# A Fourier mixing layer ahead of an MLP: twiddle factors inside the first stage's weights, and the second stage by even and odd frequencies on eight strips of the array

## The chip, the cores and the metric

The kernel runs on one core of a Trainium2 chip, in fp32 throughout. The metric is the device time of one execution in microseconds (us). Before the change it is 2734.07 us, the median of three runs (2733.72 to 2735.22).

The engines are called by their names or as the profile has them: TensorE (PE, its weight loads PEld), VectorE (DVE), ScalarE (ACT), GpSimd (POOL) and SyncE (SP), which issues most of the DMAs.

## What is computed

A global filter over the sequence in the frequency domain, followed by a two-layer MLP with a hard-swish:

```python
X = np.fft.rfft(x, axis=1)                    # x: 8 x 3008 x 256
y = np.fft.irfft(X * (filt_r + 1j * filt_i), n=3008, axis=1)
h = y.reshape(24064, 256) @ w_in              # 256 x 2048
out = (h * np.clip(h + 3, 0, 6) / 6) @ w_out  # 2048 x 256
```

## The kernel before

**The MLP and its steps.** The 24,064 tokens are cut into 47 blocks of 512 (`BLK`), the hidden width into eight parts of 256 (`NP`). Block 0 runs in a plain form while the weights are still being converted. For blocks 1 to 46 each part is one *step*: `up_1` to `up_5` make seven half-size products of 256 columns (one level of Strassen's scheme, `product`, L518), VectorE and ScalarE combine them and apply the hard-swish (L544, L549, L563, L568), `g_sums` makes the sums of the second product (L575 to L578), and `down` (L594) makes seven products in fourteen matmuls one step later. `out_1` to `out_5` add up and store a finished block. That makes 46 x 8 = 368 steps.

**The Fourier transform.** 3008 is 47 x 64, so a transform has two stages with twiddle factors between them. It is done batch by batch for batches 1 to 7, inside the steps of earlier blocks:

- `a_unit` (L349), eight per batch: the first stage, over the 47 rows of four columns of each half of the 64 columns. Four matmuls of 47x64 weights and 512 columns, on four tiles of the array (two halves of the rows, two of the columns), into two PSUM banks. ScalarE copies both banks to `t1` (L352), and `z_store` (L361) writes them to `z_tmp` in DRAM.
- `t2_load` (L365) reads `z_tmp` back in another order. `b_unit` (L372), twelve per batch, is the second stage for two of 24 indices: two full 128x128 matmuls of 256 columns into one bank. Its weights `wb` hold cosines with the twiddle factors in them, a different table for each index, and so are loaded for each batch again (`table_load`, L190) along with the filter `ft` (L187, L189).
- `f_unit` (L389 to L391) multiplies by the filter on VectorE straight from PSUM: three operations, four (L387) in batch 1. `y_unit` (L407, L408) makes the complex sum with two more, on VectorE, or in batch 1 on GpSimd (L404, L405).
- `bi_unit` (L419), six per batch: the first stage back, for four indices: four matmuls of 64x64 on 512 columns into two banks, copied by ScalarE (L422) into `t3` and written by `g_store` to `g_tmp`.
- `n_unit` (L472): the last stage, of up to five groups of 94 tokens; `t4_load` fetches its input, ScalarE copies the result into the token buffer `xn` (L478), and `t_sums` (L511) makes sums of it on GpSimd.

Batch 0 is transformed at the start in a form of its own.

**What sets the order.** There is one instruction stream per engine, written out by hand. `at(step, fn, ...)` puts a unit into a plan; the main loop emits, for each step, `up_1`, then the units that are in `EARLY` (the four with matmuls: `a_unit`, `b_unit`, `bi_unit`, `n_unit`), then the rest of the step, and at its end all other units (`f_unit`, `y_unit`, loads, stores). So a unit's matmuls stand behind `up_1`, and its VectorE work stands at the end of the step, ahead of the next step's `hswish`. `places(n)` says at which steps the units of batch n stand, `n_at` where the `n_unit`s do. For batches 2 to 7 the `b_unit`s of a batch stand two steps apart, `a_unit`s in four of eight steps.

**Buffers.** All of `a_unit`, `b_unit`, `bi_unit` and `n_unit` take their PSUM banks from one pool of two, in turn (`psF`, names `psf` and `psn`). `t1` has two buffers, `t2` three, `t3` two (`T3B`), `wb` two.

Of the kernel before, what the change touches and what calls it, by code (L numbers as in the profile page):

```python
# [10 lines left out]
FP32 = mybir.dt.float32  # L11
I32 = mybir.dt.int32
AXT = mybir.ActivationFunctionType
ALU = mybir.AluOpType
PSUM = bass.MemoryType.PSUM

# [4 lines left out]
N = 3008  # L23
NA = 47
# [12 lines left out]
NT = KH // TC  # L37
TB = 3
FB = 2
T3B = 2  # L40
NU = KH // 2
NP = DFF // 256
TOK = 2 * NA
# [12 lines left out]
def _make_tables():  # L56
    a = np.arange(NA)
    c = np.arange(NC)
    wa = np.zeros((P, P))
    wai = np.zeros((P, HC, TOK))  # L60
    start = np.zeros((P, 2 * P))
    for h in range(2):
        for k in range(KH):
            th = 2 * np.pi * ((a * k) % NA) / NA
            for g in range(2):
                wa[h * 64:h * 64 + NA, g * 64 + k] = np.cos(th)
                wa[h * 64:h * 64 + NA, g * 64 + 32 + k] = -np.sin(th)
            start[h * 64:h * 64 + NA, P + 4 * k + h] = np.cos(th)
            start[h * 64:h * 64 + NA, P + 4 * k + 2 + h] = -np.sin(th)
    wb = np.zeros((P, KH, P))  # L70
    wi = np.zeros((P, 3, NC))
    re, im = slice(0, NC), slice(NC, P)
    for k in range(KH):
        for q in range(64):
# [8 lines left out]
    for q in range(64):  # L83
        g, sign = (q, 1.0) if q < 32 else (31 - q, -1.0)
        co, si = (f([2 * np.pi * ((j * g) % NC) / NC for j in range(HC + 1)]) for f in (np.cos, np.sin))
        ab = np.concatenate([co, np.zeros(HC - 1) if q == 63 else si[1:HC]])
        wi[q, 0], wi[HALF + q, 0] = ab, sign * ab
        wi[q, 1], wi[HALF + q, 1] = ab, -ab
        wi[q, 2], wi[HALF + q, 2] = sign * ab, sign * ab
    start[:, :P] = np.eye(P)  # L90
# [17 lines left out]
            th = 2 * np.pi * (((k + NA * q if q < 32 else NA * (q - 31) - k) * n) % N) / N  # L108
            direct[q, k - KH + TC], direct[HALF + q, k - KH + TC] = 2 / N * np.cos(th), -2 / N * np.sin(th)
    f = np.float32  # L110
    return wa.astype(f), (wai / N).astype(f), wb.astype(f), wi.astype(f), start.astype(f), direct.astype(f)


@with_exitstack
def kernel(
# [8 lines left out]
):  # L124
    nc = tc.nc

    wa_np, wai_np, wb_np, wi_np, start_np, direct_np = _make_tables()
    wa_d = nc.inline_tensor(wa_np, name="wa_t").ap()
    wai_d = nc.inline_tensor(wai_np, name="wai_t").ap()
    wb_d = nc.inline_tensor(wb_np, name="wb_t").ap()  # L130
    wi_d = nc.inline_tensor(wi_np, name="wi_t").ap()
    start_d = nc.inline_tensor(start_np, name="start_t").ap()
    direct_d = nc.inline_tensor(direct_np, name="direct_t").ap()


    z_d = nc.dram_tensor("z_tmp", (B, KH, P, D), FP32, kind="Internal").ap()
    g0_d = nc.dram_tensor("g0_tmp", (NC, 2, KH, D), FP32, kind="Internal").ap()
    g_d = nc.dram_tensor("g_tmp", (B, NU, 2, 2, NC, D), FP32, kind="Internal").ap()

    def pool(name, bufs, **kw):  # L140
        return ctx.enter_context(tc.tile_pool(name=name, bufs=bufs, **kw))
# [1 line left out]
    const = pool("const", 1)  # L143
    t1p = pool("t1p", 2)
    t2p = pool("t2p", TB)
    tabp = pool("tabp", FB)
    sp = pool("sp", 2)
    yp = pool("yp", 3)
    t3p = pool("t3p", T3B)
# [7 lines left out]
    psU = pool("psU", 1, space=PSUM)  # L157
    psO = pool("psO", 1, space=PSUM)

    wa = const.tile([P, P], FP32, name="wa")  # L160
    wai = const.tile([P, HC, TOK], FP32, name="wai")
    wi = const.tile([P, 3, NC], FP32, name="wi")
    xs = const.tile([P, 3, XC, D], FP32, name="xs")
    ft = [const.tile([P, TC, D], FP32, name="ft%d" % i) for i in range(FB)]
    t4 = const.tile([P, 2 * NJ, D], FP32, name="t4")
# [12 lines left out]
    def table_load(b, c):  # L178
        if b == 0 and c >= FB:

            at = x0_at(1536 * (c - FB), 1536)
            t, wb = at[:, 0:1024].rearrange("p (k d) -> p k d", k=TC), at[:, 1024:].rearrange("p (k m) -> p k m", k=TC)
        else:
            t, wb = ft[(b * NT + c) % FB], tabp.tile([P, TC, P], FP32, name="wb")
        st["ft", b, c] = t
        for src, p0 in ((filt_r, 0), (filt_i, HALF)):
            nc.sync.dma_start(t[p0:p0 + 32, :, :].rearrange("p k d -> p (k d)"),  # L187
                              raw(src, c * TC, [[NA * D, 32], [1, TC * D]]))
            nc.sync.dma_start(t[p0 + 32:p0 + 64, :, :], raw(src, NA - c * TC, [[NA * D, 32], [-D, TC], [1, D]]))  # L189
        nc.sync.dma_start(wb, wb_d[:, ts(c, TC), :])  # L190
        st["wb", b, c] = wb
# [148 lines left out]

    def a_unit(b, c):
        xc = xs[:, (b * NB + c) % 3, :, :]
        t = t1p.tile([P, 2, XC // 2, D], FP32, name="t1")
        ps = [bank(b) for h in range(2)]
        for g in range(2):
            for h in range(2):
                nc.tensor.matmul(ps[h][ts(g, 64)], wa[ds(h * 64, NA), ts(g, 64)],  # L349
                                 xc[ds(h * 64, NA), 2 * g:2 * g + 2, :], start=True, stop=True)  # L350
        for h in range(2):
            nc.scalar.activation(out=t[:, h, :, :].rearrange("p j d -> p (j d)"), in_=ps[h], func=AXT.Copy)  # L352
        st["t1", b, c] = t

    def z_store(b, c, q=nc.gpsimd):
        t = st.pop(("t1", b, c))
        for g in range(2):
            for ri in range(2):
                p0 = g * 64 + ri * 32
                z = z_d[b, :, ts(ri, NC), :].rearrange("k (h j) d -> k h j d", h=2)  # L360
                q.dma_start(z[:, :, ds(c * XC + 2 * g, 2), :], t[p0:p0 + KH, :, :, :])  # L361

    def t2_load(b, c):
        t = t2p.tile([P, TC, D], FP32, name="t2")
        nc.sync.dma_start(t, z_d[b, ts(c, TC), :, :].rearrange("k p d -> p k d"))  # L365
        st["t2", b, c] = t

    def b_unit(b, i):
        c, r = divmod(2 * i, TC)
        ps = bank(b).rearrange("p (u d) -> p u d", u=2)  # L370
        for u in range(2):
            nc.tensor.matmul(ps[:, u, :], st["wb", b, c][:, r + u, :],  # L372
                             st["t2", b, c][:, r + u, :], start=True, stop=True)
        st["ps", b, i] = ps
# [37 lines left out]
    def bi_unit(b, i):  # L412
        ys = [st.pop(("y", b, i + v)) for v in range(2)]
        ps = [psF.tile([P, 2, D], FP32, name="psf", tag="f") for ri in range(2)]
        for v, ri in ((0, 0), (1, 0), (0, 1), (1, 1)):

            products = isinstance(ys[v], tuple)
            w, y = (wi[:, 1 + ri, :], ys[v][ri]) if products else (wi[ts(ri, 64), 0, :], ys[v][ts(ri, 64)])
            nc.tensor.matmul(ps[ri][ts(v, 64)], w, y, start=True, stop=True)  # L419
        t = t3p.tile([P, 2, 2, D], FP32, name="t3")  # L420
        for ri in range(2):
            nc.scalar.activation(out=t[:, ri, :, :], in_=ps[ri], func=AXT.Copy)  # L422
        st["t3", b, i] = t
# [260 lines left out]
    with tc.manual_schedule():  # L684
# [82 lines left out]
        direct(NU - 2)  # L767
        direct(NU - 1)
        load_bits(6)
        nc.sync.dma_start(wa, wa_d)  # L770
        n_first()
        g_store(0, NU - 4)
        for c in range(2):
# [3 lines left out]
        convert(3)  # L777

        def wai_load():
            nc.sync.dma_start(wai[:, 8:HC, :], wai_d[:, 8:HC, :])  # L780

        at(0, bi_unit, 0, NU - 2)
# [10 lines left out]
        at(2, x_load, 1, 2)  # L793

        n_at = {0: -2, 1: -2}
        used = {}
        stored = 0
        for i in range(2, len(chunks)):
            k = token(i)[0] // BLK
            head = chunks[i][1] == 0  # L800
            n_at[i] = s = (k - 1) * NP + (6 if head or k in used else 3)
            used[k] = 1
            if head:
                stored = s - 3 + (k == first[1])
            at(max(stored, n_at[i - 2] + 1), t4_load, i)
            for dh in range(2):
                at(s + dh, n_unit, i, dh)

        def places(n):
            k = first[n]
            u = [NU - 1 - i for i in range(NU)]
            b_at = [(k - 2 - j // 3) * NP + 6 - 2 * (j % 3) for j in u]

            bi_at = [b_at[i] + (5 if i % 6 == 1 else 3) for i in range(NU)]
            a_at = [(k - 7 + c // 4) * NP + (0, 2, 5, 7)[c % 4] for c in range(NB)]
            if n == 1:
                a_at = list(range(2, NB + 2))  # L820
                b_at = [12, 13, 14, 18, 19, 20, 21, 22, 26, 27, 28, 29]
                bi_at = [i + 3 for i in b_at]
            return a_at, b_at, bi_at

        prev = None
        for n in range(1, B):
            a_at, b_at, bi_at = places(n)
            for c, s in enumerate(a_at):
                at(s, a_unit, n, c)
                at(s, z_store, n, c, nc.sync if n == 1 else nc.gpsimd)  # L830
                if c >= 3:
                    at(max(a_at[c - 3], s - 6), x_load, n, c)
                elif n > 1:
                    at(max(prev[c + NB - 3], s - 6), x_load, n, c)
            for c in range(NT):
                s = b_at[2 * (c - TB) + 1] + 1 if c >= TB else a_at[-1] + 1
                at(s, t2_load, n, c)
                s = b_at[2 * (c - FB) + 1] + 1 if c >= FB else a_at[-1 if n > 1 else 3] + 1
                at(s, table_load, n, c)
            for i in range(NU):  # L840
                at(b_at[i], b_unit, n, i)
                at(b_at[i], f_unit, n, i)
                at(b_at[i] + 1, y_unit, n, i)
                if i % 2:
                    at(bi_at[i], bi_unit, n, i - 1)
                    at(bi_at[i], g_store, n, i - 1)
            prev = a_at


# [97 lines left out]
```

## Time and profile before

| | |
|---|---|
| median of three runs | 2734.07 us |
| the profiled execution's own time | 2733.72 us |
| its span, first to last instruction | 2731.9 us |
| granted TensorE clock | 0.998 |
| first step of block 1 begins | 141.15 us |
| HBM read / written | 120.86 MB / 71.93 MB |

The groups of the transform, as the page's list by line and shape has them (busy time is the union of a group's intervals; an fp32 matmul counts as two instructions):

| line | operation | count | busy us | mean ns |
|---|---|---|---|---|
| L349 | PE, `a_unit`, 47x64, 512 columns | 448 | 67.6 | 615 |
| L372 | PE, `b_unit` of batches 1 to 7, 128x128, 256 columns | 336 | 87.5 | 383 |
| L419 | PE, `bi_unit` of batches 1 to 7, 64x64, 512 columns | 336 | 48.8 | 614 |
| L472 | PE, `n_unit`, 128x128, 94 columns | 1000 | 126.2 | 272 |
| L352 | ACT, copies of `a_unit` | 112 | 60.8 | 595 |
| L389, L390, L391 | DVE, filter products of batches 2 to 7 | 72 each | 49.3, 49.1, 50.0 | 684, 683, 695 |
| L407, L408 | DVE, complex sums of batches 2 to 7 | 72 each | 49.5, 49.6 | 687, 689 |

A profile line of the timeline has the start and the length in us, the engine, the line of the kernel, the operation, the tiles written and read, shapes and a count of merged neighbours; in brackets stands how long the engine was idle ahead of it and what ended that.

### The profile page before, as it was taken

Reading aid. Unit: us, or ns where it says so; the run is one execution under the profiler, and the core shown is the slowest. Engines: PE = TensorE matmul, PEld = TensorE weight load, DVE = VectorE, ACT = ScalarE, POOL = GpSimd, SP = SyncE. Lnnn points to the kernel's source line nnn. Section 1 sums busy time; section 2 is a strip of 40 time slices with the busy share of each in tenths; the row PEclk is TensorE's granted clock in tenths of the full one; section 3 lists DMA queues with packets and bytes.
Section 4 is the critical chain, followed back from the end, with each engine's and each line's share of the span. In section 5 each row is a group of like instructions: output and inputs, shape, how many; then the busy total and the mean of one; then the engine's idle time right before and its main releaser. Section 6 shows DMA issues by size and latency. Waiting matters only on the chain.

```text
span 2731.9 us, 47123 instructions
## 1 busy us (share of the span) xinstructions
PE 2699.5 (99%) x18110; PEld 2400.5 (88%) x18110; DVE 1953.9 (72%) x3395; ACT 1328.3 (49%) x2662; POOL 423.7 (16%) x622
## 2 busy tenths in 40 slices
PE   8999999999999999999999999999999999999998
PEld 6488889998899988999889998899988989999997
DVE  7968756787567875678757777577775777766665
ACT  3344454445544455444554444544455454444443
POOL 2433321001210012100121001210012000100000
PEclk9999999999999999999999999999999999999999
DMA  8632233212332123321233212332123321100000
GB/s 234 198 106 83 55 85 89 72 50 56 85 92 68 50 57 92 100 63 41 61 88 98 70 40 57 91 93 70 40 60 90 91 73 39 42 24 24 19 9 16
DMA packets 119645, 195.88 MB, mean 72 GB/s; under 512 B 21561, under 2 KB 82681, under 8 KB 119105
## 3 DMA queue, kind: packets, MB, share of 16 engines
q1 hardware_dynamic: 101663, 148.19, 18.9%
q0 software_dynamic: 17152, 44.23, 7.0%
q8 instruction: 143, 2.34, 0.4%
q14 instruction: 81, 0.66, 0.1%
q10 hardware_dynamic: 606, 0.46, 0.1%
HBM read 120.86 MB, written 71.93 MB: 71 GB/s over the span
## 4 chain that ended last, share of the span: by engine, by line
PE 94%; DVE 4%; DMA 1%; issue 1%; ACT 0%; SPq 0%; POOL 0%; POOLq 0%; DVEq 0%
PE po L594 42%; PE al L518 23%; PE be L518 17%; PE psn L472 4%; PE psf L372 2%; PE psf L419 2%; PE psf L349 2%; DVE s L387 1%; DVE g L568 1%; PE po L318 1%; PE po L372 0%; DVE y L243 0%; DVE y L254 0%; DVE y L256 0%; DVE w_all L259 0%
## 5 line engine op out<-in xcount | busy, mean ns | idle before, releaser
L594 PEld LDWEIGHTS po<-w_all,g 128*128 128x128 f32 x10304 | 1368.1, 191 | 142.2 <-issue 38.1
L594 PE MATMUL po<-w_all,g 128*128 128x128 f32 x10304 | 1399.4, 276 | 0.8 <-DVE g L568 0.6
L568 DVE SCALAR_TENSOR_TENSOR g<-r,h 128x512 f32<-128x512 f32 x736 | 511.8, 695 | 275.2 <-ACT r L563 263.5
L563 ACT ACTIVATE r<-h,half_c 128x512 f32<-128x512 f32 x736 | 531.0, 721 | 330.8 <-DVE h L544 318.7
L518 PE MATMUL al<-xt,w_all 128*128 128x256 f32 x2208 | 660.4, 381 | 3.9 <-DVE h L549 3.4
L518 PE MATMUL be<-xn,w_all 128*128 128x256 f32 x1472 | 437.8, 379 | 0.0
L544 DVE TENSOR_TENSOR h<-be,s 128x512 f32<-128x512 f32 x368 | 254.1, 691 | 252.1 <-PE be L518 242.3
L518 PEld LDWEIGHTS al<-xt,w_all 128*128 128x128 f32 x2208 | 335.3, 192 | 6.5 <-DVE h L549 4.7
L518 PEld LDWEIGHTS be<-xn,w_all 128*128 128x128 f32 x1472 | 279.7, 190 | 37.9
L558 ACT ACTIVATE h<-al 128x256 f32<-128x256 f32 x368 | 141.0, 383 | 347.5 <-PE al L518 347.5
L549 DVE TENSOR_TENSOR h<-al,s 128x256 f32<-128x256 f32 x368 | 156.1, 424 | 164.0 <-PE al L518 162.6
L576 DVE TENSOR_TENSOR g<-g 128x512 f32<-128x512 f32 x368 | 257.1, 699 | 12.7
L539 ACT ACTIVATE s<-al 128x256 f32<-128x256 f32 x368 | 141.2, 384 | 198.5 <-PE al L518 198.5
L530 ACT ACTIVATE s<-be 128x256 f32<-128x256 f32 x368 | 141.0, 383 | 176.7 <-PE be L518 176.7
L518 PE MATMUL al<-xn,w_all 128*128 128x256 f32 x736 | 219.9, 381 | 0.5 <-ACT h L558 0.5
L518 PE MATMUL be<-xt,w_all 128*128 128x256 f32 x736 | 218.9, 379 | 0.0
L529 ACT ACTIVATE s<-al 128x256 f32<-128x256 f32 x368 | 141.0, 383 | 71.4 <-PE al L518 71.4
L361 POOL DMA_DIRECT2D z_tmp<-t x192 | 110.8, 581 | 414.2 <-ACT t L352 411.8
L575 DVE TENSOR_TENSOR g<-g 128x256 f32<-128x256 f32 x368 | 162.5, 442 | 12.6
L578 DVE TENSOR_TENSOR g<-g 128x256 f32<-128x256 f32 x368 | 161.0, 437 | 12.5
L518 PEld LDWEIGHTS be<-xt,w_all 128*128 128x128 f32 x736 | 139.8, 190 | 18.9
L650 POOL TENSOR_TENSOR o<-p,o 128x256 f32<-128x256 f32 x45 | 32.7, 726 | 794.1 <-ACT t L422 397.7
(138 smaller groups left out, 1902.3 us busy)
## 6 DMA issues: line engine op xcount, KB each, us to landing
g_tmp<-t POOLq DMA_DIRECT2D x96, 256.0 KB, 3.8
t<-g_tmp SPq DMA_DIRECT2D x188, 120.0 KB
t<-z_tmp SPq DMA_DIRECT2D x42, 512.0 KB
z_tmp<-t POOLq DMA_DIRECT2D x192, 96.0 KB, 3.1
out_dram<-o SPq DMA_DIRECT2D x321, 47.0 KB
xs<-in_x_dram SPq DMA_DIRECT2D x112, 128.0 KB
ft<-in_filt_r_dram SPq DMA_DIRECT2D x88, 128.0 KB
ft<-in_filt_i_dram SPq DMA_DIRECT2D x88, 128.0 KB
```

The source lines that it names most:

```text
L518: nc.tensor.matmul(ps, w_in[p][:, w, :], x, start=start, stop=stop, skip_group_check=True)
L529: nc.scalar.activation(out=s[:, 0, :], in_=al, func=AXT.Copy)
L530: nc.scalar.activation(out=s5, in_=be[:, 1, :], func=AXT.Copy)
L539: nc.scalar.activation(out=s[:, 1, :], in_=al, func=AXT.Copy)
L544: nc.vector.tensor_tensor(out=st["h"][0].rearrange("p (a n) -> p a n", a=2), in0=be, in1=s, op=ALU.add)
L549: nc.vector.tensor_tensor(out=st["h"][1][:, 256:512], in0=al, in1=s5, op=ALU.add)
L563: nc.scalar.activation(out=r, in_=st["h"][i], func=AXT.Relu, bias=half_c, scale=1.0 / 6.0)
L568: nc.vector.scalar_tensor_tensor(out=st["g", k, p][:, o:o + 2, :].rearrange("p a n -> p (a n)"), in0=st["r", i], scalar=1.0, in1=st["h"][i ...
L575: v.tensor_tensor(out=g[:, G1, :], in0=g[:, G3, :], in1=g[:, G22, :], op=ALU.add)
L576: v.tensor_tensor(out=g[:, G3:G2 + 1:2, :], in0=g[:, G3:G1 + 1, :], in1=g[:, G11:G11 + 1, :].broadcast_to([P, 2, 256]), op=ALU.subtract)
L578: v.tensor_tensor(out=g[:, G4, :], in0=g[:, G12, :], in1=g[:, G2, :], op=ALU.subtract)
L594: nc.tensor.matmul(st["po", k][bank][:, part, u, :], g[:, a, ts(u, P)], w_out[p][:, w, :], start=(p == 0 and n in OPENS and u == 0), stop= ...
```

## The change

The twiddle factors move from the second stage's weights into the first stage's. Each of the 64 columns gets a table of its own in the first stage: `wa` grows from 128 to 1552 columns, and `a_unit` makes eight matmuls of 256 columns in place of four of 512. The second stage is then the same for every index: a constant table `wf` takes the place of `wb` for batches 1 to 7. The columns j and j + 32 are added and subtracted ahead of it, which splits the output frequencies into even and odd ones. For batches 2 to 7 the sums are made behind the first stage (`a_sums`: ScalarE copies one bank, VectorE adds and subtracts the other); for batch 1 behind `t2_load` (`t2_sums`, from the raw halves). `b_unit` then handles two units (four indices) with eight matmuls of 64x32 weights and 512 columns, on eight strips of the array, into two banks. The order of rows in `ft` follows (even, then odd frequencies), so each filter chunk is loaded by eight DMAs and no table load. `z_tmp` has another layout. `t3` gets one buffer, and for batch 0 half of its tiles come from `t1`'s pool. The steps are placed anew: `b_unit` at every second step of `f_at`, an `f_unit` in two steps running, `a_unit` in odd steps, `n_unit` in steps that depend on the kind of block. `bi_unit`, `f_unit`, `y_unit` and `n_unit` compute as before.

```diff
-T3B = 2
+T3B = 1
...
+            at = k // 4 * 4 + (0, 2, 1, 3)[k % 4]
+            for j in range(HC):
+                tw = 2 * np.pi * (((a * NC + h * HC + j) * k) % N) / N
+                wa[h * 64:h * 64 + NA, j * 2 * KH + at] = np.cos(tw)
+                wa[h * 64:h * 64 + NA, j * 2 * KH + KH + at] = -np.sin(tw)
...
     def a_unit(b, c):
         xc = xs[:, (b * NB + c) % 3, :, :]
-        t = t1p.tile([P, 2, XC // 2, D], FP32, name="t1")
-        ps = [bank(b) for h in range(2)]
-        for g in range(2):
-            for h in range(2):
-                nc.tensor.matmul(ps[h][ts(g, 64)], wa[ds(h * 64, NA), ts(g, 64)],
-                                 xc[ds(h * 64, NA), 2 * g:2 * g + 2, :], start=True, stop=True)
-        for h in range(2):
-            nc.scalar.activation(out=t[:, h, :, :].rearrange("p j d -> p (j d)"), in_=ps[h], func=AXT.Copy)
-        st["t1", b, c] = t
+        t = t1p.tile([P, XC // 2, 2, D], FP32, name="t1")
+        ps = [bank(b).rearrange("p (j d) -> p j d", d=D) for h in range(2)]
+        for j in range(2):
+            for g in range(2):
+                for h in range(2):
+                    nc.tensor.matmul(ps[h][ts(g, 64), j, :], wa[ds(h * 64, NA), ds((c * XC + 2 * g + j) * 2 * KH, 64)],
+                                     xc[ds(h * 64, NA), 2 * g + j, :], start=True, stop=True)
+        for h in range(2 if b == 1 else 1):
+            nc.scalar.activation(out=t[:, :, h, :], in_=ps[h], func=AXT.Copy)
+        st["t1", b, c] = t, ps[1]
+
+    def a_sums(b, c):
+        t, ps = st["t1", b, c]
+        nc.vector.tensor_tensor(out=t[:, :, 1, :], in0=t[:, :, 0, :], in1=ps, op=ALU.subtract)
+        nc.vector.tensor_tensor(out=t[:, :, 0, :], in0=t[:, :, 0, :], in1=ps, op=ALU.add)
+
+    def t2_sums(b, c):
+        t = st["t2", b, c]
+        u = st["t2", b, c] = t1p.tile([P, XC // 2, 2, D], FP32, name="t1")
+        nc.vector.tensor_tensor(out=u[:, :, 0, :], in0=t[:, :, 0, :], in1=t[:, :, 1, :], op=ALU.add)
+        nc.vector.tensor_tensor(out=u[:, :, 1, :], in0=t[:, :, 0, :], in1=t[:, :, 1, :], op=ALU.subtract)
...
     def b_unit(b, i):
         c, r = divmod(2 * i, TC)
+        if b:
+            t = st.pop(("t2", b, c))
+            ps = [bank(b) for k in range(2)]
+            for s_ in range(2):
+                for ri in range(2):
+                    for k in range(2):
+                        nc.tensor.matmul(ps[k][ds(ri * 64 + s_ * 32, 32)].rearrange("p (v d) -> p v d", v=2),
+                                         wf[ts(k, 64), s_, ts(ri, 32)], t[ts(k, 64), :, s_, :], start=True, stop=True)
+            for k in range(2):
+                st["ps", b, i + k] = ps[k].rearrange("p (u d) -> p u d", u=2)
+            return
...
-        t = t3p.tile([P, 2, 2, D], FP32, name="t3")
+        t = (t3p if b or i & 2 else t1p).tile([P, 2, 2, D], FP32, name="t3" if b or i & 2 else "t1")
...
-        nc.sync.dma_start(wa, wa_d)
+        nc.sync.dma_start(wa[:, 0:528], wa_d[:, 0:528])
+        nc.sync.dma_start(wf, wf_d)
...
         def wai_load():
+            nc.sync.dma_start(wa[:, 528:], wa_d[:, 528:])
             nc.sync.dma_start(wai[:, 8:HC, :], wai_d[:, 8:HC, :])
...
+        N_AT = {"a": ((2, 4), (2, 4), (6, 6)), "A": ((4, 5), (1, 1), (4, 5)), "B": ((2, 3), (1, 1), (2, 3))}
+        N_FIRST = {0: ((3, 4),), 1: ((), (2, 2), (3, 3)), 2: ((2, 2),), 3: ((1, 1),)}
...
             if n == 1:
-                a_at = list(range(2, NB + 2))
-                b_at = [12, 13, 14, 18, 19, 20, 21, 22, 26, 27, 28, 29]
-                bi_at = [i + 3 for i in b_at]
-            return a_at, b_at, bi_at
-
+                f_at = [12, 13, 14, 15, 19, 20, 21, 22, 26, 27, 28, 29]
+                return list(range(2, NB + 2)), f_at, [f + 1 for f in f_at], [16, 17, 23, 24, 30, 31]
+            k = first[n] * NP
+            a_at = [k - 7 * NP + i for i in (1, 3, 5, 7, 9, 11, 13, 15)]
+            f_at, y_at, bi_at = ([k - (5 - 2 * r) * NP + i for r in range(2) for i in p]
+                                 for p in ((2, 3, 6, 7, 12, 13), (4, 5, 10, 11, 14, 15), (8, 14, 16)))
+            return a_at, f_at, y_at, bi_at
+
+        sums_at = [11, 11, 17, 18, 25, 25]
...
             for i in range(NU):
-                at(b_at[i], b_unit, n, i)
-                at(b_at[i], f_unit, n, i)
-                at(b_at[i] + 1, y_unit, n, i)
-                if i % 2:
-                    at(bi_at[i], bi_unit, n, i - 1)
-                    at(bi_at[i], g_store, n, i - 1)
+                if i % 2 == 0:
+                    at(f_at[i], b_unit, n, i)
+                    at(bi_at[i // 2], bi_unit, n, i)
+                    at(bi_at[i // 2], g_store, n, i)
+                at(f_at[i], f_unit, n, i)
+                at(y_at[i], y_unit, n, i)
```

## The prediction

> **What bounds it.** I read the page's busy rows first, then the chain that ended last, the groups by shape, and the timeline of TensorE and VectorE around single steps.
>
> ```profile
> PE 2699.5 (99%) x18110; PEld 2400.5 (88%) x18110; DVE 1953.9 (72%) x3395; ACT 1328.3 (49%) x2662; POOL 423.7 (16%) x622
> ...
> PE 94%; DVE 4%; DMA 1%; issue 1%; ACT 0%; SPq 0%; POOL 0%; POOLq 0%; DVEq 0%
> ```
>
> TensorE holds 94% of the chain, VectorE 4%. So from about 330 us on a saving counts only if it shortens TensorE's own row of matmuls; a cost on VectorE counts only when it makes TensorE wait. The timeline gives the price of each piece, since a step runs from one `al<-xn` (the first product of `up_1`) to the next:
>
> ```profile
> 1160.76 0.60 PE L518 MATMUL al<-xn,w_all 128*128 128x256 f32 x2
> ...
> 1162.05 1.03 PE L372 MATMUL psf<-t,wb 128*128 128x256 f32 x4
> ...
> 1167.77 0.60 PE L518 MATMUL al<-xn,w_all 128*128 128x256 f32 x2
> ...
> 1173.91 0.60 PE L518 MATMUL al<-xn,w_all 128*128 128x256 f32 x2
> ```
>
> A bare step takes 6.15 us (1167.77 to 1173.91), one with a `b_unit` 7.01: 0.864 us each. Likewise 1099.03 to 1106.39 with an `a_unit` is 7.36, so 1.217; a `bi_unit` also 1.217, a five-column `n_unit` 1.117. These sums hold to 0.01 us in nearly all 368 steps; where a step is longer, TensorE waited.
>
> VectorE has a gap in each bare step, and the trace shows what an `f_unit` in that gap does:
>
> ```profile
> 1113.02 0.69 DVE L568 SCALAR_TENSOR_TENSOR g<-r,h 128x512 f32<-128x512 f32 x1 [1.47 <-ACT r L563]
> ...
> 1166.69 0.69 DVE L389 TENSOR_TENSOR s<-psf,ft 128x512 f32<-128x512 f32 x1
> ...
> 1168.09 0.69 DVE L391 TENSOR_TENSOR s<-psf,ft 64x512 f32<-64x512 f32 x1
> ...
> 1168.81 0.69 DVE L568 SCALAR_TENSOR_TENSOR g<-r,h 128x512 f32<-128x512 f32 x1
> ...
> 1171.90 0.42 DVE L549 TENSOR_TENSOR h<-al,s 128x256 f32<-128x256 f32 x1
> ```
>
> The gap is 1.47 us; the three products take 2.09 and end 1.02 us into the next step. That step still takes 6.15: the `h` sum (L549) ends at 1172.32, in time for `up_5` at 1172.59. There are 0.3 us to spare.
>
> **Strips (TensorE).** Batches 1 to 7 have 84 `b_unit`s of two full-array matmuls. The change makes 42 of them, each eight matmuls of 64x32 on 512 columns. Before, a pair cost 2 x 0.864 = 1.728 us. No eight-strip group is in the trace; the nearest row is the four-tile one, L349, also 64-wide with 512 columns: 1.217 us, its four matmuls starting 7 ns apart. If eight run as four do, the price is 1.217 + 4 x 0.007 = 1.245. Lower bound 1.2; upper bound two rounds of four: the second passes of L349 start 0.48 us after the first, so 512 columns stream in about 0.85, and 1.217 + 0.85 = 2.07.
> Here a rule speaks against the change. The Trainium skill ("TensorEngine Tiling (Array Packing)", Key Properties) says that changing the tiling mode drains the array. The row agrees and prices it: 1.217 against 0.85 of streaming, 0.36 per visit, which the full-array `b_unit` does not pay (0.864 for 512 columns in all). Streaming alone would give 42 x (1.728 - 0.88) = 36 us; with the drain it is 42 x (1.728 - 1.245) = 20.3 us. I take 20.3. That eight overlap at all rests on "TensorE: Matmul & The Clock Gate", Part 3, which reports 16 tiles together at 10.6 times one; no run here shows it, hence a rival.
>
> **First stage (TensorE).** `a_unit` has eight matmuls of 256 columns instead of four of 512: the same columns on the same four tiles. Twice the weight loads, each of 64 columns (131 ns in L349's PEld row, four side by side) under 213 ns of streaming: 0. If they showed, 56 x 0.1 = 6 us; below nothing is excluded, no column goes away.
>
> **Step placement.** Six steps now hold an `a_unit` and a five-column `n_unit`, and take 9.23 us, not 6.15 + 1.217 + 1.117 = 8.48: the second unit waits for one of the two `psf` banks. A seventh, at 328.66, holds `bi_unit` and `a_unit`: 1.06 us too long. In the built order of the changed kernel no step holds two such units. Gain 6 x 0.75 + 1.06 = 5.6 us.
>
> **Bank waits.** `b_unit` now fills both `psf` banks, freed by two `f_unit`s in two consecutive steps. The page on tiling (Restrictions and Gotchas) says that row tiles may not use one bank together, so two banks are forced. The price is in this trace, in batch 1:
>
> ```profile
> 259.43 2.81 DVE L387 TENSOR_TENSOR s<-psf,ft 64x512 f32<-64x512 f32 x4
> ...
> 261.24 2.13 PE L419 MATMUL psf<-y,wi 64*64 64x512 f32 x8
> ```
>
> That step starts at 259.85; `f_unit` ends at 262.24, 2.39 us in, and the step is 1.04 too long: the wait is the end minus 1.35. For batches 2 to 7: the first `f_unit` ends 1.02 us in; in the bare step after it the second starts where L407 does now (1173.39), runs 2.09, and ends at 1175.48, 1.57 into the following step. If that step has a `bi_unit`, it waits 1.57 - 1.35 = 0.22. The order shows this four times a batch: 24 x 0.22 = 5.3 us lost. Behind the waiting TensorE stand the products of that step, and behind them ScalarE and VectorE; the third pair meets an `n_unit` that takes the bank freed earlier: 0. Bounds 0 and 24 x 0.6 = 14.
>
> **VectorE sums.** `a_sums` adds 96 operations of about 0.69 us in 48 steps, 1.38 per step in the 1.47 gap, in steps where TensorE has 1.217 more: 0, as the two `y` operations (L407, L408) cost nothing in the same place. Without that cover up to 48 x 0.6. ScalarE loses 48 copies of 0.595 us: nobody waits for it.
>
> **Batch 1.** There VectorE already delays TensorE: between 179 and 323 us the steps are 10.2 us longer than their parts. The change keeps four products of 2.81 us per `f_unit`, now in three runs of four steps, and adds 12 sums (8.3 us). In a run the odd `f_unit` ends 1.8 us into a bare step; the `h` sum follows its start by 3.09, ends at 5.36 where 4.82 is allowed: 0.55 lost. The even one ends about 2.45 into a step with `b_unit` or `bi_unit`: 1.1. Per run 2 x (0.55 + 1.1) = 3.3, three runs 10. The first sums also wait for `t2` loads, issued now at 168.42 to 169.40 and due at about 170.5: 0 to 5, I take 3. So 13 instead of 10.2: 3 lost (bounds -3 and +8). `t3` with one buffer makes ScalarE wait for `g_store` (3.8 us to landing, after some 4 us): batch 1's visits in adjacent steps, 7 us apart, just fit.
>
> **Transfers.** 42 loads of the second-stage table, 256 KB each, go: 10.8 MB. They hide now (DMA share 0.26 in the middle stages; TensorE never waits for `wb`): 0. Each filter chunk has eight issues on SP instead of four and a table load: 3 x 0.42 us more per chunk, no one queued behind is late. The first-stage table grows from 64 KB to about 1 MB, 786 KB of it ahead of `wai` at 77.9 us; `wai` is first used at 92.7 and VectorE's weight conversion bounds that stage: 0, at most 3.
>
> **Sum.** 20.3 + 5.6 - 5.3 - 3 = 17.6 us off the profiled execution's 2733.72 (span 2731.9 plus 1.8 around it; 0.35 below the median 2734.07): 2716.
>
> **Rivals.**
> *Strips in two rounds* (slower): eight 64x32 strips need four streams for each half of the rows; L349 proves two. At 2.07 us a visit the strips lose 42 x 0.34 = 14.4 and the sum is 2733.7 + 14.4 - 5.6 + 8.3 = 2751. It turns slower once a visit costs over 1.66 us (42 x 0.065 pays the 2.7 us that waits cost net). Against it: the four of L349 start and end together. Chance 0.09.
> *VectorE becomes the bound*: in an `f_unit` pair its work is 4.08 + 2.09 = 6.17 us in a bare step of 6.15. If the 0.3 us of room fails, 36 pairs lose 0.3 to 0.6 each, 11 to 22 us: 2727 to 2738. For it: batch 1 shows it. Against it: after one `f_unit` the step stayed 6.15, and a step with 1.1 to 1.2 more on TensorE follows each pair. Chance 0.13.
> *Waits all hide*: 20.3 + 5.6: 2708. Chance 0.13. My forecast has 0.65, and by itself lies in 2711 to 2722.
>
> **Numbers.** 2705 to 2732 leaves out the first rival and part of the second, some 0.13. A measurement of this kernel tells 0.2%, 5.5 us, from no change; so faster 0.85, same 0.06, slower 0.09.
>
> **What would show it.** Steps with strips at 7.39 us with eight matmuls starting within 0.1 us (8.2 with two groups: the first rival). Bare steps after a strip step at 6.15 (longer with a wait for L549's sum: the second). `bi_unit` steps right after an `f_unit` at 7.6, others at 7.365. No step at 9.23. The stretch 141 to 329 us about as long as now. The forecast fails if strips do not overlap, or if the two banks stay busy longer than I traced.

## The result and the profile after

The changed kernel takes 2719.31 us (median of four runs, 2718.32 to 2722.81), against 2734.64 for the kernel before (four runs, 2733.72 to 2738.78); the ratio is 0.9943 (95% interval 0.9926 to 0.9961). The profiled execution took 2718.84 us, with a span of 2717.1. The forecast was 2716, in a range of 2705 to 2732.

The same two rows of the page, after (engine: busy time, share of the span and instructions; then the chain by engine):

```profile
PE 2681.4 (99%) x18894; PEld 2358.1 (87%) x18894; DVE 2033.3 (75%) x3503; ACT 1308.0 (48%) x2614; POOL 407.4 (15%) x622
...
PE 92%; DVE 5%; issue 1%; DMA 0%; ACT 0%; SPq 0%; POOL 0%; DVEq 0%; POOLq 0%
```

TensorE is 18 us less busy and VectorE 79 us more, yet the kernel got faster: TensorE still holds 92% of the chain, and VectorE's share of it rose from 4% to 5%. Where it rose comes below.

A step with strips, in the timeline of the changed kernel, with the step behind it and the first filter products:

```profile
1159.15 0.60 PE L575 MATMUL al<-xn,w_all 128*128 128x256 f32 x2
...
1160.54 1.09 PE L422 MATMUL psf<-t,wf 64*32 64x512 f32 x16
...
1165.44 0.68 DVE L446 TENSOR_TENSOR s<-psf,ft 128x512 f32<-128x512 f32 x1
...
1166.51 0.60 PE L575 MATMUL al<-xn,w_all 128*128 128x256 f32 x2
...
1166.83 0.69 DVE L448 TENSOR_TENSOR s<-psf,ft 64x512 f32<-64x512 f32 x1
...
1170.65 0.42 DVE L606 TENSOR_TENSOR h<-al,s 128x256 f32<-128x256 f32 x1
...
1172.66 0.60 PE L575 MATMUL al<-xn,w_all 128*128 128x256 f32 x2
```

1159.15 to 1166.51 is 7.36 us, so a visit of eight strips costs 1.217 us, exactly what the four-tile `a_unit` cost before. In the records the eight first passes start within 47 ns, 7 ns apart, and the eight second passes follow 0.45 us later in the same way. The bare step behind, 1166.51 to 1172.66, takes 6.15 us although a filter unit ends in it: the `h` sum (L606) is over at 1171.07, ahead of `up_5`.

The two traces can be set against each other step by step. A step's *wait* is its length less its parts: 6.148 us bare, 0.864 per `b_unit` before, 1.217 per strip visit, `a_unit` or `bi_unit`, 1.117 per five-column `n_unit`. Nearly all 368 steps have none, in either kernel.

| where | predicted | measured |
|---|---|---|
| start up to the first step | 0, at most +3 | -0.5 |
| second stage, 84 x 0.864 to 42 x 1.217 | -20.3 | -21.5 |
| steps that two units with two banks shared | -5.6 | -5.6 |
| bank waits of `bi_unit`, batches 2 to 7 | +5.3 | +2.6 |
| waits in batch 1, 10.2 before | +3 | +11.1, to 21.3 |
| behind the last step | 0 | -1.3 |
| sum, us | -17.6 | -15.2 (the spans: -14.8) |

The total was right to 3 us of 17.6, and part of that is luck. Batch 1 lost 8.1 us more than forecast. Four rows came out 5.7 us better, among them the start and the end, which the forecast had at nothing; 0.4 us are in no row. The gain at the end lies behind the last issue of a store, and its cause stays open. Batch 1's term was almost four times its size and outside its own bound of 8. The experiments look for its cause; some test the other terms.

### The profile page after: what moved, and what is told of

Its sections match the earlier page's. It is cut to its first block, busy times and chain, and to the rows that moved or that the text cites. A ratio compares the mean times of both kernels' runs of the same rounds, so it can differ in the third digit from the quotient of the medians.

```text
span 2717.1 us, 49001 instructions
## 1 busy us (share of the span) xinstructions
PE 2681.4 (99%) x18894; PEld 2358.1 (87%) x18894; DVE 2033.3 (75%) x3503; ACT 1308.0 (48%) x2614; POOL 407.4 (15%) x622
## 4 chain that ended last, share of the span: by engine, by line
PE 92%; DVE 5%; issue 1%; DMA 0%; ACT 0%; SPq 0%; POOL 0%; DVEq 0%; POOLq 0%
PE po L651 42%; PE al L575 23%; PE be L575 17%; PE psn L529 4%; PE psf L476 2%; PE psf L379 2%; PE psf L422 1%; DVE g L625 1%; DVE s L444 1%; PE po L346 1%; DMA out_dram<-o 0%; DVE g L632 0%; DVE y L271 0%; PE po L429 0%; DVE y L282 0%
## 5 line engine op out<-in xcount | busy, mean ns | idle before, releaser
L606 DVE TENSOR_TENSOR h<-al,s 128x256 f32<-128x256 f32 x368 | 156.1, 424 | 161.0 <-PE al L575 159.8
L635 DVE TENSOR_TENSOR g<-g 128x256 f32<-128x256 f32 x368 | 169.7, 461 | 12.5
L632 DVE TENSOR_TENSOR g<-g 128x256 f32<-128x256 f32 x368 | 164.2, 446 | 12.6
L402 POOL DMA_DIRECT2D z_tmp<-t x192 | 95.3, 503 | 452.2 <-DVE t L389 441.9
L496 POOL DMA_DIRECT2D g_tmp<-t x84 | 52.5, 630 | 644.9 <-ACT t L479 644.9
```

Source lines behind the costliest of these rows:

```text
L606: nc.vector.tensor_tensor(out=st["h"][1][:, 256:512], in0=al, in1=s5, op=ALU.add)
L632: v.tensor_tensor(out=g[:, G1, :], in0=g[:, G3, :], in1=g[:, G22, :], op=ALU.add)
L635: v.tensor_tensor(out=g[:, G4, :], in0=g[:, G12, :], in1=g[:, G2, :], op=ALU.subtract)
```

## The experiments

The start of the first step lies between 140.4 and 145.1 us in the profiled executions of these kernels, whatever was edited in the later steps, while steps that an edit did not touch agree within some 0.03 us, but for a few single ones that differ by up to 0.24. So the verdicts on single terms rest on step lengths and waits, not on medians.

**e1: the complex sums of batch 1 on VectorE.**

```diff
     def near(b):
-        return b == 1
+        return False
```

> The complex sums of batch 1 go from GpSimd to VectorE, in the form that batches 2 to 7 have (three filter products and two sums per unit in place of four products). Theory (GpSimd's sums hold VectorE up: in the changed kernel two VectorE operations that run beside one of them take 1.21 and 1.37 us in place of 0.70 and 0.44, so 1.45 us per unit): VectorE's work per step of a run falls from 4.08 + 2.81 + 1.45 = 8.3 to 4.08 + 2.09 + 1.38 = 7.55 us, the 21 us of waits of batch 1 fall to about 15: some 2713 us. Rival (only the amount of VectorE's own work counts): it rises from 6.9 to 7.55 us per step of a run, 12 times 0.65: some 8 us slower, 2727 us.

Measured: 2716.75 us (ratio to the kernel before 0.9931, 0.9914 to 0.9947). The waits of batch 1 fell from 21.3 to 17.1 us. VectorE does more operations by itself and TensorE waits less, so the rival, which made it slower, falls. The size was 2 us off: with both the filter products and the sums in one step, `f_unit` ends later, and the next `bi_unit` waits 1.87 for its bank in place of 1.04.

**e2: the twelve t2 sums left out.**

```diff
-                if n == 1:
-                    at(sums_at[c], t2_sums, n, c)
```

> Leaves out the twelve sums of batch 1 (t2_sums), so that its second stage reads the raw halves. If the sums are a main part of what batch 1 lost: 8.3 us of VectorE work gone from a stretch that it bounds, 6 to 8 us less, 2712 us. If the waits come from the runs of four filter steps with GpSimd beside them: only the 0.7 us of the first step with strips and a part of the steps behind it go, 1 to 3 us less, 2717 us.

Measured: 2719.28 us; waits of batch 1 19.8. The sums cost 1.5 us: the 0.67 of the first step with strips, and 0.8 of the step behind it. They are not the main cause, and the 3 us that the prediction gave the first of them were too many.

**e3: pairs with a free step, in place of runs of four.**

```diff
-                f_at = [12, 13, 14, 15, 19, 20, 21, 22, 26, 27, 28, 29]
-                return list(range(2, NB + 2)), f_at, [f + 1 for f in f_at], [16, 17, 23, 24, 30, 31]
+                f_at = [12, 13, 15, 16, 19, 20, 22, 23, 26, 27, 29, 30]
+                return list(range(2, NB + 2)), f_at, [f + 1 for f in f_at], [17, 21, 24, 28, 31, 32]
...
-        sums_at = [11, 11, 17, 18, 25, 25]
+        sums_at = [11, 14, 17, 21, 25, 28]
```

> Batch 1's filter steps stand in pairs with a free step behind each, in place of runs of four; the rest as in the changed kernel. If the length of the runs made the waits: 21 us of waits fall to 10 or less, 2708 us. If GpSimd beside VectorE makes them (the free step has GpSimd's sum in it too, and no more matmuls than a bare one): each pair still loses about 1.8 in its second step and about 2 in the free one, so within 3 us of the changed kernel, 2716 to 2722 us.

Measured: 2719.06 us; waits of batch 1 19.9. The step behind each first filter step still loses about 1.8 in five of six cases (1.3 in the first). So the length of the runs is not the cause either.

**e7: GpSimd writes zeros in place of its two sums.** This is the test of the cause itself. The zeros depend on no product, so GpSimd writes them earlier, up to three at once; beside the operations in question it then does nothing.

```diff
-            nc.gpsimd.tensor_tensor(out=y[re], in0=s1[re], in1=s2[re], op=ALU.subtract)
-            nc.gpsimd.tensor_tensor(out=y[im], in0=s1[im], in1=s2[im], op=ALU.add)
+            nc.gpsimd.memset(y, 0.0)
```

> Leaves out batch 1's complex sums: GpSimd writes zeros to y in place of its two sums, and reads no SBUF operand. The rest as in the changed kernel, with the four products and runs of four. If GpSimd's reading sums are what slows VectorE: the operations beside them go back to 0.70 and 0.43 us, and batch 1's waits fall from 21.3 to the 10 to 13 us that the prediction had reckoned without that. If the amount of VectorE's work alone makes the waits: 21 us as before.

Measured: 2712.39 us in one run; waits of batch 1 10.4 us. First the changed kernel, then e7, at the same step of batch 1 (VectorE and GpSimd in the timeline):

```profile
240.75 1.26 POOL L461 TENSOR_TENSOR y<-s,s 64x512 f32<-64x512 f32 x1 [10.36 <-DVE s L444]
241.35 1.21 DVE L625 SCALAR_TENSOR_TENSOR g<-r,h 128x512 f32<-128x512 f32 x1
242.08 1.60 POOL L462 TENSOR_TENSOR y<-s,s 64x512 f32<-64x512 f32 x1
242.59 1.37 DVE L632 TENSOR_TENSOR g<-g 128x256 f32<-128x256 f32 x1
```

```profile
239.62 2.79 DVE L444 TENSOR_TENSOR s<-psf,ft 64x512 f32<-64x512 f32 x4
242.44 0.69 DVE L624 SCALAR_TENSOR_TENSOR g<-r,h 128x512 f32<-128x512 f32 x1
243.17 0.42 DVE L631 TENSOR_TENSOR g<-g 128x256 f32<-128x256 f32 x1
```

With GpSimd's sums, the hard-swish takes 1.21 us and the first sum of `g_sums` 1.37; without, 0.69 and 0.42. The difference is 1.47 us, and the step's wait falls from 1.85 to 0.35. In the second run of four the waits become 0.35 + 1.05 + 0.35 + 1.04 in place of 1.85 + 1.29 + 2.51 + 1.04, and the third run is the same within 0.1. (The 2.51 is more than 1.85 because VectorE came 0.67 us later out of the step before, which was stretched too.) VectorE's own operations and their placement are unchanged, so GpSimd's two sums make half of batch 1's waits.

Where the zeros do fall beside VectorE, they slow nothing. In e7, with a hard-swish and a t2 sum, both on two SBUF operands:

```profile
231.45 1.46 POOL L461 MEMSET y<- 128x512 f32 x3
231.66 0.68 DVE L624 SCALAR_TENSOR_TENSOR g<-r,h 128x512 f32<-128x512 f32 x1
232.26 0.68 DVE L394 TENSOR_TENSOR t<-t 128x512 f32<-128x512 f32 x1
```

The first run is another matter, in e7 as in the changed kernel: more of GpSimd's work stands beside it. These are lines of the changed kernel:

```profile
168.54 0.73 POOL L568 TENSOR_TENSOR xt<-xn 128x256 f32<-128x256 f32 x1 [33.45 <-ACT xn L535]
...
171.78 15.48 POOL L293 TENSOR_TENSOR w_all<-w_all 128x128 f32<-128x128 f32 x24
...
184.66 0.83 DVE L625 SCALAR_TENSOR_TENSOR g<-r,h 128x512 f32<-128x512 f32 x1
185.52 0.56 DVE L632 TENSOR_TENSOR g<-g 128x256 f32<-128x256 f32 x1
```

GpSimd's sums of the weights (L293; L265 before) were over at 149.5 us in the kernel before. With the `n_unit`s placed anew, 24 of them stand behind token sums that wait for the result of an `n_unit` (the 33.45 us in brackets), and run to 187.3. Beside them the hard-swish takes 0.83 us in place of 0.69, and a sum of `g_sums` 0.56 in place of 0.42. No run took them out, so their part of the 0.67 and 1.7 us lost in steps 12 and 13 is not known.

**e6: VectorE alone, and its work spread.** The cause told where a better version might be: no sums on GpSimd, both complex sums of a pair in a free step that holds a `bi_unit`, and the t2 sums in steps with two `n_unit`s.

```diff
-        return b == 1
+        return False
...
+                f_at = [12, 13, 15, 16, 19, 20, 22, 23, 26, 27, 29, 30]
+                y_at = [14, 14, 17, 17, 21, 21, 24, 24, 28, 28, 31, 31]
+                return list(range(2, NB + 2)), f_at, y_at, [17, 21, 24, 28, 31, 32]
...
+        sums_at = [11, 11, 18, 18, 25, 25]
```

> Batch 1 with the sums on VectorE, filter steps in pairs, both complex sums of a pair in the free step behind it, bi_unit of the pair before in that free step too, and the t2 sums in steps 11, 18 and 25, which hold two n_units each. VectorE's work is then 6.17 us in the two filter steps (7.37 and 6.15 us of matmuls) and 6.84 in the free one (7.37). Theory: with GpSimd off VectorE's back and its work spread so, batch 1's waits fall from 21.3 to about 4 (first sums waiting for their load, 0.1 at each bi_unit): 17 us less than the changed kernel, 2702 us. Rival (the two banks and the load of t2 keep batch 1 late whatever VectorE does): over 12 us of waits stay, 2711 us.

Measured: 2706.14 us (2705.39 to 2707.91; ratio to the kernel before 0.9891, 0.9875 to 0.9908). That is below every run of the changed kernel. The waits of batch 1 are 9.1 us: not the 4 of the theory, and not the over 12 of the rival. Step 25 alone (counted from block 0, as in `f_at`), with the output sums of a block, four t2 sums and GpSimd's token sums, loses 3.8. Three lines of that step:

```profile
272.34 1.03 DVE L625 SCALAR_TENSOR_TENSOR g<-r,h 128x512 f32<-128x512 f32 x1
...
276.82 0.67 DVE L601 TENSOR_TENSOR h<-be,s 128x512 f32<-128x512 f32 x1
276.95 1.75 PE L651 MATMUL po<-w_all,g 128*128 128x128 f32 x8 [1.87 <-DVE o L706]
```

The step begins at 268.70; its hard-swish starts 3.64 us in, where 0.5 to 0.6 is usual, and is stretched to 1.03, this time beside the token sums.

**e10: the same with step 25 relieved.**

```diff
-                y_at = [14, 14, 17, 17, 21, 21, 24, 24, 28, 28, 31, 31]
+                y_at = [14, 14, 17, 17, 21, 21, 25, 25, 28, 28, 31, 31]
...
-        sums_at = [11, 11, 18, 18, 25, 25]
+        sums_at = [11, 11, 18, 18, 24, 24]
```

> As e6_spread, but the four complex sums that stood in step 24 go to step 25, and the t2 sums of step 25 to step 24. In e6_spread step 25 lost 3.8 us and step 32 0.5: VectorE came 3.6 us late out of step 24, and the block's output sums and GpSimd's token sums fell on top. Theory: VectorE then has 8.1 us of work in step 25 where TensorE has 8.4, and the loss falls below 1 us: 3 us less than e6_spread, 2703 us. If it is the token sums of GpSimd (four in that step) that cost it: half of the 3.8 us stays.

Measured: 2706.93 us (2705.67 to 2708.65; ratio 0.9897, 0.9882 to 0.9912). Step 25 now loses 1.24, more than the theory's 1 and less than the half of 3.8 that the rival left, so neither is settled: the token sums still stretch VectorE's operations there (a sum of `g_sums` takes 0.83 us). The waits of batch 1 are 7.0 in place of 9.1; the 0.5 of step 32 stays. In the time this can't be told from e6: the profiled execution's first step began at 142.8 against 140.4 us. The gain of 2 us is seen in the steps alone.

**e4: the `n_unit`s placed as before.**

```diff
-        N_AT = {"a": ((2, 4), (2, 4), (6, 6)), "A": ((4, 5), (1, 1), (4, 5)), "B": ((2, 3), (1, 1), (2, 3))}
+        N_AT = {"a": ((2, 4), (2, 4), (6, 7)), "A": ((4, 5), (1, 1), (4, 5)), "B": ((2, 3), (1, 1), (2, 3))}
...
-                steps = (6, 6)
+                steps = (6, 7)
```

> The two halves of the third n_unit of a block stand in steps 6 and 7 again, as before the change, so that six steps hold an a_unit and an n_unit. Theory: each of the six loses 0.75 us to the two banks, as the kernel before showed: 4.5 us slower, 2724 us. Rival: with one of the two banks of a_unit now freed by VectorE later than ScalarE freed it, the wait is longer, 1.5 us or more each, 2728 us or more. If the new placement gave nothing: 2719 us.

Measured: 2724.90 us (ratio 0.9961, 0.9946 to 0.9976). Six steps take 9.233 us again, a wait of 0.75 each, to the hundredth what the kernel before had. The term of the sum is settled, and the later release by VectorE adds nothing.

**e5: the sums of batches 2 to 7 left out.** ScalarE copies both banks again (`for h in range(2)`), and the line `at(s, a_sums, n, c)` is gone.

> Leaves out the 96 sums and differences of batches 2 to 7 (a_sums), so that ScalarE copies both banks and z_tmp holds the raw halves. Theory (they fit VectorE's gap of 1.47 us per step): no step of batches 2 to 7 changes, the waits there stay at 2.6 us in all. Rival (VectorE is near the bound): the 0.1 us waits of bi_unit and others vanish, and the time falls by 3 to 10 us.

Measured: 2719.33 us in one run; the waits behind step 32 are 2.7 us, against 3.0 in the changed kernel's trace and 2.7 in that of e8, which has the sums. Steps with an `a_unit` take 7.370 us with the sums and without. The 66 us of added VectorE work cost nothing where they stand.

**e8: the old table loaded again.**

```diff
+            nc.sync.dma_start(tabp.tile([P, TC, P], FP32, name="wb"), wb_d[:, ts(c, TC), :])
             return
```

> Loads the old second-stage table again with each filter chunk of batches 1 to 7 (42 loads of 256 KB, into a buffer that nothing reads). Theory: the 10.8 MB that the change took away were hidden, so no step changes and the time stays within the noise of a single run. Rival: SyncE's queue or the DMA engines then bring t2 and ft late, and steps with strips or filter products wait: some us more.

Measured: 2719.64 us in one run; waits 21.3 in batch 1 and 2.7 behind it, as without but for one step of batch 6 that is 0.23 us shorter. The transfers that the change took away had cost nothing as transfers. (Nothing reads the tables here, so a wait for one is not tried; TensorE shows none in the trace of before.)

**e9: four tiles in place of eight strips.**

```diff
-                for ri in range(2):
-                    for k in range(2):
-                        nc.tensor.matmul(ps[k][ds(ri * 64 + s_ * 32, 32)].rearrange("p (v d) -> p v d", v=2),
-                                         wf[ts(k, 64), s_, ts(ri, 32)], t[ts(k, 64), :, s_, :], start=True, stop=True)
+                for k in range(2):
+                    nc.tensor.matmul(ps[k][ts(s_, 64)].rearrange("p (v d) -> p v d", v=2),
+                                     wf[ts(k, 64), s_, :], t[ts(k, 64), :, s_, :], start=True, stop=True)
```

> Batches 1 to 7: the second stage on four tiles of 64x64 (real and imaginary part of one parity side by side) in place of eight strips of 64x32. The same columns and the same rows of weights, but the rows of the result stand in another order than the filter's, so that what follows multiplies rows that do not belong together. Theory (eight strips run all at once, like four tiles): a step with the second stage stays at 7.37 us, the time within 1 us of the changed kernel by the steps. Rival (the eight strips are partly one after another, or their sixteen issues show): 42 steps become 0.03 to 0.1 us or more shorter, 1 to 4 us.

Measured: 2719.43 us. The groups by line and shape, first of the changed kernel, then of e9 (busy us, mean ns):

```profile
L422 PE MATMUL psf<-t,wf 64*32 64x512 f32 x672 | 48.9, 601 | 1.0 <-DVE s L444 1.0
```

```profile
L421 PE MATMUL psf<-t,wf 64*64 64x512 f32 x336 | 48.9, 614 | 1.0 <-DVE s L443 1.0
```

Twice the instructions, the same 48.9 us, and no step shorter. Eight strips cost what four tiles do. So the strips as such save no time: they put the rows of the result in the filter's order, real parts in the upper half and imaginary parts in the lower. What saves is the split by parity with one table for all indices: a 128x128 matrix per index becomes two of 64x64, half the multiplications, and four such matrices work side by side. Four indices take 512 columns of the array's time in place of 1024.

## Why the prediction was right, and where not

**Strips: right.** The price of 1.217 + 4 x 0.007 was 0.03 too high per visit; the four more issues do not show, as e9 confirms. The 0.36 us that a visit takes beyond its streaming (1.217 against 0.85) was priced right by the row of the four-tile unit. The prediction put it down to the drain of the tiling mode; no run tells the drain from other costs of a visit, such as its first weight load. The rival with two rounds (2.07 us) is refuted by the length of the steps, 7.365 us.

**First stage: right.** An `a_unit` with twice the weight loads takes 7.370 us in its step against 7.365, 0.3 us in all.

**Placement: right**, 5.6 us, and e4 gives 0.75 per step back. That the same placement would move GpSimd's sums of the weights into batch 1 was not seen.

**Bank waits: right mechanism, half the size.** The second filter unit of a pair ends at 1174.10, 1.44 us into its next step and not 1.57, because its start is earlier than the row that I took (1172.01 is 5.50 into its step, 1173.39 was 5.62):

```profile
1172.01 0.69 DVE L446 TENSOR_TENSOR s<-psf,ft 128x512 f32<-128x512 f32 x1
...
1172.66 0.60 PE L575 MATMUL al<-xn,w_all 128*128 128x256 f32 x2
...
1173.41 0.69 DVE L448 TENSOR_TENSOR s<-psf,ft 64x512 f32<-64x512 f32 x1
...
1174.05 1.18 PE L476 MATMUL psf<-y,wi 64*64 64x512 f32 x8
```

1.44 - 1.35 is 0.09, and that is the wait of nearly every one of the 24 steps. The rule from batch 1 held; the 0.13 of start time made the other half.

**VectorE's sums and the transfers: right**, both at nothing (e5, e8). The first-stage table is 0.79 MB and not about 1 MB, which changed nothing. The rival in which VectorE becomes the bound came true in batch 1 and nowhere else: the bare steps behind strips stayed at 6.148 in batches 2 to 7.

**Batch 1: the step that failed.** The prediction put "0.55 lost" for the bare step behind the first and the third filter unit of a run, 1.1 for the step behind the second and the fourth, and 3 us for the first t2 sums. In the second and third run the bare steps lost 1.8 and 2.5, the others 1.3 and 1.0; the t2 sums cost 1.5. With GpSimd's sums out of the way (e7) the same steps lose 0.35, 1.05, 0.35 and 1.04, and the whole is 10.4 of the 13 that the prediction had worked out: it had reckoned a VectorE that nobody disturbs. The mistake could have been seen in the trace of before, at the step from 251.18, which is 1.65 us too long:

```profile
253.03 1.26 POOL L404 TENSOR_TENSOR y<-s,s 64x512 f32<-64x512 f32 x1 [2.72 <-DVE s L387]
253.63 1.21 DVE L568 SCALAR_TENSOR_TENSOR g<-r,h 128x512 f32<-128x512 f32 x1
254.36 1.60 POOL L405 TENSOR_TENSOR y<-s,s 64x512 f32<-64x512 f32 x1
254.87 1.38 DVE L575 TENSOR_TENSOR g<-g 128x256 f32<-128x256 f32 x1
```

I took the durations from a bare step of batch 4, where GpSimd is idle, and used them in batch 1, where it is not. In the kernel before, all twelve steps behind a filter unit also had a `b_unit`, `n_unit` or `bi_unit` on TensorE, 0.86 to 2.1 us that covered part of the loss: from step 19 on, steps with `b_unit` and `n_unit` (1.98 us) lost 0.14 to 0.28, those with a `b_unit` alone 1.65 and 1.66. The change packs two units into one visit, and so leaves six of the twelve bare. The cover went, and the loss that it hid came out; this is read from the two traces, and no run gives the cover back alone. Of the 27 us that strips and placement saved, 11 were given back there.

The Trainium skill ("SBUF — State Buffer", section "SBUF: two separate sides") says that VectorE operations with two SBUF inputs and GpSimd operations that read SBUF share one pair of ports, and that who comes second is held until the first is done. The traces fit it. The hard-swish and the sums of `g_sums` read two SBUF operands and are stretched; the filter products read PSUM and take 0.685 us beside GpSimd's sums and 0.687 without; the zeros of e7, for which GpSimd reads nothing, leave a hard-swish beside them at 0.68. GpSimd is held too: in both traces its second sum takes 1.60 us where it starts while a hard-swish is running (20 of 24), and 1.26 us where none is (4 of 24). That the ports are the reason is the page's statement; that GpSimd's sums are what stretches VectorE is shown by e7.

**What stays open.** The 10.4 us of waits left in e7 are of three kinds: lost in the step behind a filter unit (0.35), at a bank (1.04), and in steps 12 and 13 (2.4 together). The first two fit the reckoning but were not tried one by one; of the third, e2 shows that the t2 sums make 1.5 in the changed kernel, and the part of GpSimd's sums of the weights is open. Of e6's and e10's remaining 7 to 9 us, step 25 was tried and the rest was not.

## What to carry to other kernels

Where every step's length is the sum of its TensorE parts, work out the price of each part from steps that differ by it, and forecast by counting. When a change takes TensorE work out of a step, look in that very step for what the work had covered: another engine's delay that had cost nothing there can now bound the step, even if that engine is a quarter idle on the whole. And take an engine's durations from the stage where they will be used: here the sums given to GpSimd cost VectorE 1.47 us beside them, more than the 1.38 us of doing them itself. When units move, see also what stands behind them in the streams of the other engines.

## What was not expected of the hardware

Eight fp32 matmuls on 64x32 strips cost the same 1.217 us as four on 64x64 tiles, with sixteen instructions in place of eight. GpSimd operations of 1.26 and 1.60 us on 64 partitions stretched two VectorE operations by 0.52 and 0.95 us, while products from PSUM beside them kept their 0.685 us.
